# Attention with routing to experts: the written order inside a pair of heads, who empties PSUM, and the remainder keys' product with v as two tiles of 64 columns

## The chip, the cores and the metric

The kernel runs on one core of a Trainium2 chip. The core has TensorE (PE, with its weight loads listed apart as PEld), VectorE (DVE), ScalarE (ACT), GpSimd (POOL) and SyncE (SP), which issues most transfers. The metric is device microseconds of one launch, smaller is better.

## What is computed

Attention over 8 batches, 8 heads, 576 positions and head size 64 with a bias that a small network makes of positions; then each of the 4608 tokens goes to the one of 8 experts that a gate picks. Cut to what matters:

```python
scores = scale * q @ k.T + bias            # (8, 8, 576, 576)
attn = exp(scores - max); attn /= attn.sum(-1)
x = (attn @ v), heads side by side          # (4608, 512)
logits = x @ w_gate + modality_bias[modality_id]
e = argmax(logits); gate = softmax(logits)[e]
out = gate * (relu(x @ w1[e]) @ w2[e])
```

## The kernel before

**Stages.** A bias table is built first (to about 76 us of the span), then `attention()` works through 32 pairs of heads (4 pairs a batch) to about 643 us, then the experts' tiles follow. Beside the pairs runs the routing of the batch that is just done.

**A pair.** The 576 positions of a pair are 512 in four blocks of 128 rows for each of its two heads (units u = 0 to 3) and a remainder of 64 rows for each head, both heads together (u = 4). For each unit `scores` (L435) multiplies q with k in three terms of a split into a high and a low part. For u < 4 it works in tiles of 64 rows, one head in each, twelve products of 288 columns; for u = 4 in full rows, six. DVE adds the bias table and takes the row minimum (L449, the scores are negated), ACT takes the exponential in place (`exps`, L464), both from `Eb`, a ring of four tiles. `etrans` (L479, L485, L490) transposes the exponentials on PE into the PSUM banks `eps`, part 0 and part 1, and `take` copies them to `eT`. The columns 512 to 576 of a unit (the remainder keys) are copied together by POOL (`compact`, L469) and transposed by `rtrans` (L507) into `rT`. `prep` transposes q and k of a later pair (L403, and L408 with L409 for the remainders), and `take` writes them in a high (`ph0`, `ph1`, `ph2`) and a low part.

**The products with v.** `av(n, half, part)` makes one output of 128 rows (64 of each head) and 288 positions in two parts. The products with the 512 main keys (L527) are column tiles: 128 rows by 64 columns, one head in each, so two stand side by side. The remainder keys of both heads are the 128 rows of one product (L521), with `vrem`, a 128 by 128 matrix that has each head's v in its own corner and zeros elsewhere. It comes first in half 0 and last in half 1. In the trace each of these float32 products has two records, each transpose has one.

**What sets the order.** `ORDER` is written out by hand, one string for each unit. PE, ACT, DVE and POOL each take their instructions in that order. The letters: `S` scores; `e`, `f` the exponentials of the first and second head; `t`, `T` the two parts of `etrans` of the unit two before; `R` is `rtrans`; `a`, `A`, `b`, `c` the four parts of `av` for the pair before; `0`, `1`, `2` are `prep` of the next pair; `C` is `compact`; `X` and `B` are one step of routing with PE work and one without; `q`, `k` turn q and k of the pair after the next on POOL; `V`, `L` start loads on SP. A number behind a letter puts off its copies out of PSUM by so many letters (they also run when their bank is wanted again). `ON_ACT` names the copies that ACT makes; DVE makes the others.

Of the kernel before, what the change touches and what calls it, by code (L numbers as in the profile page):

```python
# [22 lines left out]
S = 576  # L23
# [87 lines left out]
class Attn:  # L111
# [205 lines left out]
        self.flush(lambda x: x[1] == ("x", self.n_x % 2))  # L317
        return self.xps[self.n_x % 2]

    ON_ACT = ("av0", "av1", "e01", "e20", "e21", "e30", "e31", "e40", "e41", "lt0", "lt1", "rT", "xr")  # L320

    def take(self, what, out, ps, scale=1.0):

# [6 lines left out]
    def take_now(self, what, out, ps, scale):  # L330

        if what[:2] == "pl":
            ps, hi = ps
            self.nc.vector.scalar_tensor_tensor(out, ps, scale, hi.bitcast(F32), op0=ALU.mult, op1=ALU.subtract)
        elif what in self.ON_ACT:
            self.nc.scalar.activation(out, ps, AF.Copy, scale=scale)  # L336
# [173 lines left out]
    def av(self, n, half, part):  # L510

        nc = self.nc
        if half == 0 and part == 0:
            self.xT[n] = self.xTb[n // NP % 2][:, n % NP, :]
        if part == 0:
            self.avps = self.xbank()
        v = self.vmain[n]
        sl = slice(HS * half, HS * half + HS)
        ps = self.avps[:, 0:HS]

        rem = lambda **kw: nc.tensor.matmul(ps, self.vrem[n % 2], self.rT[:, sl], skip_group_check=True, **kw)  # L521
        if half == 0 and part == 0:
            rem(start=True, stop=False)
        for k in (0, 1) if part == 0 else (2, 3):
            for h in range(2):
                o = slice(64 * h, 64 * h + 64)
                nc.tensor.matmul(  # L527
                    ps[o, :],
                    v[:, h, k, :],
                    self.eT[:, h, k, sl],  # L530
                    start=half == 1 and k == 0,
                    stop=half == 0 and k == 3,
                    tile_position=(0, 64 * h),
                    skip_group_check=True,
                )
        if part == 1:
            if half == 1:
                rem(start=False, stop=True)
            self.take(f"av{half}", self.xT[n][:, sl], ps)
            self.avps = None  # L540
            if half == 1:
                del self.vmain[n]

    def first_steps(self, route):
# [34 lines left out]


    ORDER = (
# [5 lines left out]
    )  # L587

    def attention(self):
# [889 lines left out]
```

## Time and profile before

| | |
|---|---|
| median of 3 runs | 1091.09 us (1089.97 to 1091.13) |
| the profiled execution | 1091.33 us, its span 1089.4 us |
| PE busy | 1066.4 us, 98% of the span |
| DVE, ACT, POOL busy | 736.7, 678.8, 246.6 us |
| granted clock of TensorE | 0.999 |

The span runs from the first to the last instruction; 1.9 us of the launch lie around it. Matmuls overlap, so a busy PE is read best from the starts of its groups: what a group costs is the time from its start to the start of the next one.

### The profile page before, as it was taken

The numbers are of one execution on the slowest core, as the hardware profiler recorded it, in microseconds if no ns is written. First come the engines' busy times: TensorE is split into PE (matmuls) and PEld (weight loads), VectorE is DVE, ScalarE is ACT, GpSimd is POOL, SyncE is SP. The second block draws the span as 40 slices with busy tenths as digits, with TensorE's granted clock in tenths as the row PEclk, the third lists the DMA queues.
The fourth block names the chain that finished last, engine by engine and source line by source line (L and its number), as shares of the span: only waits on it lengthen the run. The fifth ranks groups of instructions, "written<-read, shape, count | busy, mean of one in ns | idle before, by whom it ended". The sixth has DMA issues, their size and how long they took to land.

```text
span 1089.4 us, 23080 instructions
## 1 busy us (share of the span) xinstructions
PE 1066.4 (98%) x8580; PEld 842.9 (77%) x8580; DVE 736.7 (68%) x1580; ACT 678.8 (62%) x1333; POOL 246.6 (23%) x521
## 2 busy tenths in 40 slices
PE   6989999999999999999999999999999999999997
PEld 3456777777777777777776779999999999898986
DVE  7987768677686776766868756587455665545544
ACT  6776766767667667676676765654455554444544
POOL 1012222414224224142242221331110001101110
PEclk9999999999999999999999999999999999999999
DMA  5983412212212122222221511112113621151500
GB/s 164 219 192 116 144 43 77 69 56 74 69 52 92 54 67 69 55 84 60 56 88 49 201 45 40 59 64 70 58 49 117 240 100 52 38 215 48 195 31 32
DMA packets 71960, 98.19 MB, mean 90 GB/s; under 512 B 23054, under 2 KB 47886, under 8 KB 71842
## 3 DMA queue, kind: packets, MB, share of 16 engines
q1 hardware_dynamic: 65826, 77.62, 24.0%
q0 software_dynamic: 5920, 19.03, 4.8%
q8 instruction: 69, 1.13, 0.4%
q14 instruction: 49, 0.40, 0.1%
q10 hardware_dynamic: 96, 0.00, 0.0%
HBM read 135.62 MB, written 23.90 MB: 146 GB/s over the span
## 4 chain that ended last, share of the span: by engine, by line
PE 90%; DVE 1%; issue 1%; ACT 1%; POOL 0%; POOLq 0%; DVEq 0%; ACTq 0%
PE p L1200 18%; PE p L1217 18%; PE sps L435 14%; PE xps L527 13%; PE eps L479 10%; PE xps L521 4%; PE xps L403 3%; PE xps L872 2%; PE xps L1180 2%; PE xps L507 1%; PE eps L485 1%; PE xps L779 1%; PE xps L409 1%; DVE Eb L449 1%; PE p L1399 1%
## 5 line engine op out<-in xcount | busy, mean ns | idle before, releaser
L464 ACT ACTIVATE Eb<-Eb,mn 128x576 f32<-128x576 f32 x288 | 221.1, 770 | 37.2 <-DVE mn L449 36.8
L449 DVE CUSTOM_DVE_ANT_0 Eb<-sps,NBm 128x576 f32<-128x576 f32 x256 | 183.7, 755 | 83.2 <-PE sps L435 70.3
L435 PE MATMUL sps<-QK 64*128 64x288 f32 (+1 forms) x1728 | 172.8, 311 | 3.1 <-DVE mn L449 2.0
L435 PEld LDWEIGHTS sps<-QK 64*128 64x128 f32 (+1 forms) x1728 | 133.4, 185 | 44.3 <-DVE QK L338 16.4
L1200 PE MATMUL p<-QK,w1hi 128*128 128x256 f32 x1136 | 160.9, 284 | 0.0
L1203 DVE SCALAR_TENSOR_TENSOR hl<-p,hh 128x512 fp32r<-128x512 f32 x72 | 49.7, 691 | 154.5 <-ACT hh L1202 154.5
L527 PE MATMUL xps<-eT,vraw 128*64 128x288 f32 x1024 | 151.8, 418 | 0.0
L1200 PEld LDWEIGHTS p<-QK,w1hi 128*128 128x128 f32 x1136 | 147.0, 192 | 2.9 <-issue 1.8
L479 PE MATMUL eps<-idf,Eb 128*128 128x128 f32 x1024 | 143.9, 276 | 0.0
L479 PEld LDWEIGHTS eps<-idf,Eb 128*128 128x128 f32 x1024 | 115.6, 141 | 12.7 <-issue 5.7
L336 ACT ACTIVATE eT<-eps 128x512 f32<-128x512 f32 x192 | 106.6, 590 | 28.8 <-PE eps L479 15.2
L1202 ACT ACTIVATE hh<-p 128x512 fp32r<-128x512 f32 x72 | 43.0, 598 | 116.6 <-PE p L1200 112.6
L1217 PE MATMUL p<-w2hi,hh 128*128 128x512 f32 x288 | 114.2, 396 | 0.0
L1217 PE MATMUL p<-w2hi,hl 128*128 128x512 f32 x288 | 112.5, 391 | 0.0
L1226 POOL DMA_INDIRECT out<-mo,idt x36 | 38.5, 1069 | 322.4 <-ACT QK L1183 222.2
L469 POOL COPY rem<-Eb 128x128 f32<-128x128 f32 x128 | 37.8, 296 | 301.8 <-ACT Eb L464 226.4
L527 PEld LDWEIGHTS xps<-eT,vraw 128*64 128x64 f32 x1024 | 62.2, 136 | 53.5 <-issue 25.4
L1163 DVE TENSOR_TENSOR w2lo<-NBm,w2hi 128x1024 fp32r<-128x1024 f32 x72 | 88.2, 1225 | 16.2 <-ACT w2hi L1162 16.1
L1200 PE MATMUL p<-QK,w1lo 128*128 128x256 f32 x568 | 91.3, 283 | 0.0
L1163 DVE TENSOR_TENSOR w1lo<-NBm,w1hi 128x1024 fp32r<-128x1024 f32 x72 | 84.2, 1231 | 0.2 <-ACT w1hi L1162 0.2
L1225 ACT ACTIVATE mo<-p,gates 128x512 f32<-128x512 f32 x36 | 24.8, 689 | 89.1 <-PE p L1217 74.4
L1200 PEld LDWEIGHTS p<-QK,w1lo 128*128 128x128 f32 x568 | 78.3, 192 | 0.0
(221 smaller groups left out, 1685.7 us busy)
## 6 DMA issues: line engine op xcount, KB each, us to landing
NBm<-moe_w SPq DMA_DIRECT2D x23, 2048.0 KB
NBm<-moe_w SPq DMA_DIRECT2D x44, 1024.0 KB
NBr<-xg SPq DMA_DIRECT2D x20, 516.0 KB
NBm<-xTb SPq DMA_DIRECT2D x32, 288.0 KB
qraw<-q SPq DMA_DIRECT2D x32, 256.0 KB
kraw<-k SPq DMA_DIRECT2D x32, 256.0 KB
vraw<-v SPq DMA_DIRECT2D x32, 256.0 KB
xg<-blank SPq DMA_DIRECT2D x9, 516.0 KB
```

Source lines behind the costliest of these rows:

```text
L336: self.nc.scalar.activation(out, ps, AF.Copy, scale=scale)
L435: nc.tensor.matmul(self.sps[h][:, half, 0:HS], QK[o, q, qs], QK[o, k, HS * half : HS * half + HS], start=i == 0, stop=i == 2, skip_group_c ...
L449: nc.vector.tensor_tensor_reduce(out=e.rearrange("p (t w) -> p t w", t=2), in0=self.sps[h][:, :, 0:HS], in1=nb.rearrange("p (t w) -> p t w ...
L464: self.nc.scalar.activation(e, e, AF.Exp, bias=mn, scale=-1.0, accum_out=sm)
L479: nc.tensor.transpose(ps[:, k, :], e[:, part, P * k : P * k + P], self.idf)
L521: rem = lambda **kw: nc.tensor.matmul(ps, self.vrem[n % 2], self.rT[:, sl], skip_group_check=True, **kw)
L527: nc.tensor.matmul(ps[o, :], v[:, h, k, :], self.eT[:, h, k, sl], start=half == 1 and k == 0, stop=half == 0 and k == 3, tile_position=(0, ...
L1163: self.nc.vector.tensor_tensor(l, w, h.bitcast(F32), op=ALU.subtract)
L1200: nc.tensor.matmul(ps[:, a, :], w[:, c, fs], x[:, c, :], start=i == 0, stop=i == len(ops) - 1)
L1202: nc.scalar.activation(hh[:, sl, :], ps, AF.Relu)
L1203: nc.vector.scalar_tensor_tensor(hl[:, sl, :], ps, 0.0, hh[:, sl, :].bitcast(F32), op0=ALU.max, op1=ALU.subtract)
L1217: nc.tensor.matmul(ps, h[:, f, sl], m[:, f, :], start=i == 0, stop=i == len(ops) - 1)
```

## The change

Three things change. The remainder product is written as two column tiles of 64, as the other products with v are. `ORDER` has the letters in other places: in u = 0 and 1 `1` (L403) stands between `S` and `a` and no longer between `T` and `A`; `t` of the last unit stands before `S`; the routing steps `X` stand in u = 2, 3 and 4, of which none is ahead of `t` in u = 0 any more; `B` comes four times instead of five; `k` and `L` are a unit earlier and later, `V` a unit later. `ON_ACT` gives `e00`, `e11`, `ph0`, `ph1`, `ph2` to ACT and `e01`, `e31`, `e40`, `e41`, `lt0`, `xr` to DVE.

```diff
-    ON_ACT = ("av0", "av1", "e01", "e20", "e21", "e30", "e31", "e40", "e41", "lt0", "lt1", "rT", "xr")
+    ON_ACT = ("av0", "av1", "e00", "e11", "e20", "e21", "e30", "lt1", "ph0", "ph1", "ph2", "rT")
...
-        rem = lambda **kw: nc.tensor.matmul(ps, self.vrem[n % 2], self.rT[:, sl], skip_group_check=True, **kw)
+        def rem(**kw):
+            for h in range(2):
+                o = slice(64 * h, 64 * h + 64)
+                nc.tensor.matmul(
+                    ps[o, :], self.vrem[n % 2][:, o], self.rT[:, sl], tile_position=(0, 64 * h), skip_group_check=True, **kw
+                )
...
     ORDER = (
-        "S X B t R1 T3 f e C L",
-        "01 t3 S a T 11 A f e C",
-        "S B t2 X e f k C q T2",
-        "b S e c B t1 T2 f V C",
-        "S B X 2 t T e B",
+        "S B t 01 R1 e f T2 C",
+        "t1 S 12 L a k T1 f B e C A2",
+        "q S t1 e T2 X B f C b",
+        "B S c1 e T X f t C",
+        "B S 2 t2 V T2 X e",
     )
```

On PE, in u = 1 of a pair in the middle, the first half of the products with v stood like this between two units' scores:

```order
L435 MATMUL sps_724<-QK_73 128x288
L521 MATMUL xps_78<-rT,vrem_110 128x288
L527 MATMUL xps_78<-eT,vraw_3687 64x288 x4
L490 MATMUL eps_726<-idf,Eb 64x64 x2
L403 MATMUL xps_77<-idf,qks_109 128x128 x4
L527 MATMUL xps_78<-eT,vraw_3687 64x288 x4
L435 MATMUL sps_723<-QK_73 128x288
```

Now it stands like this (the products' line is L533 now, the remainder's L524):

```order
L435 MATMUL sps_724<-QK_73 128x288
L403 MATMUL xps_78<-idf,qks_109 128x128 x4
L524 MATMUL xps_77<-rT,vrem_110 64x288 x2
L533 MATMUL xps_77<-eT,vraw_3732 64x288 x4
L490 MATMUL eps_726<-idf,Eb 64x64 x2
L533 MATMUL xps_77<-eT,vraw_3732 64x288 x4
L435 MATMUL sps_723<-QK_73 128x288
```

The transposes of k (L403) moved ahead of the products, which now run in column tiles from the remainder to the last one.

On PE, in u = 3, the end of the second half and what follows up to the remainder rows' scores (six products of L435 in a row) was this:

```order
L435 MATMUL sps_724<-QK_73 128x288
L527 MATMUL xps_77<-eT,vraw_3687 64x288 x4
L521 MATMUL xps_77<-rT,vrem_110 128x288
L479 MATMUL eps_725<-idf,Eb 128x128 x4
L479 MATMUL eps_726<-idf,Eb 128x128 x4
L435 MATMUL sps_723<-QK_73 128x288 x6
L872 MATMUL xps_78<-idf,xTb_94 128x128 x4
L408 MATMUL xps_77<-idf,krem_3771 128x64
```

and is this now (L878 was L872):

```order
L435 MATMUL sps_724<-QK_73 128x288
L533 MATMUL xps_77<-eT,vraw_3732 64x288 x4
L524 MATMUL xps_77<-rT,vrem_110 64x288 x2
L479 MATMUL eps_726<-idf,Eb 128x128 x4
L878 MATMUL xps_78<-idf,xTb_94 128x128 x4
L479 MATMUL eps_725<-idf,Eb 128x128 x4
L435 MATMUL sps_723<-QK_73 128x288 x6
L408 MATMUL xps_77<-idf,krem_3818 128x64
```

The routing's transposes (L872) moved from behind the scores to between the two parts of `etrans`, whose parts changed places.

On DVE, at the end of the first pair after a batch, the minimum of the last unit (`mn_4_0`), two routing steps (L803, L811, then L818 to L821) and the remainder's high and low parts (L338 and L334 on `QK_72`) stood like this ahead of the next pair's first minimum (`mn_0_0`):

```order
L449 ISA Eb,mn_4_0_3700<-sps_723,NBr 128x576
L449 ISA mn_4_0_3700 128x1
L803 TENSOR_TENSOR lw_3631<-xps_77,rec 128x64
L811 TENSOR_REDUCE lgs_3704<-lw_3631 128x40
L338 CAST QK_72<-xps_78 128x192
L334 SCALAR_TENSOR_TENSOR QK_72<-xps_78,QK_72 128x192
L818 TENSOR_TENSOR lgs_3704<-lgs_3704,mbias 128x40
L820 TENSOR_REDUCE mx_3722<-lgs_3704 128x5
L821 TENSOR_TENSOR lgs_3704<-lgs_3704,mx_3722 128x40
L449 ISA Eb,mn_0_0_3738<-sps_723,NBm 128x576
```

and now (L809 was L803, L817 was L811):

```order
L449 ISA Eb,mn_4_0_3722<-sps_723,NBr 128x576
L449 ISA mn_4_0_3722 128x1
L334 SCALAR_TENSOR_TENSOR QK_72<-xps_77,QK_72 128x192
L809 TENSOR_TENSOR lw_3702<-xps_78,rec 128x64
L817 TENSOR_REDUCE lgs_3743<-lw_3702 128x40
L449 ISA Eb,mn_0_0_3760<-sps_723,NBm 128x576
```

The remainder's low part moved ahead of the routing, its high part left DVE, and L818 to L821 went behind the next unit's minima.

## Rows read from the trace of the kernel before

**Rows 1.** Busy time by engine from 300 to 400 us, PE clock, DMA share, GB/s.

```profile
core 0: us, PE busy (x) PEld busy (x) DVE busy (x) ACT busy (x) POOL busy (x), PEclk, DMA share, GB/s
300.00:400.00 100.00, 99.82 (x857) 73.33 (x856) 74.59 (x203) 69.75 (x167) 29.72 (x64) 1.00 0.22 64
```

**Rows 2.** Waits of PE from 100 to 690 us: total, times, longest.

```profile
PE xps L507 <- DVE QK L1184: 1.6, 1, 1.6
PE sps L435 <- DVE QK L338: 0.5, 1, 0.5
```

**Rows 3.** Timeline of PE, one pair: start us, length, line, operation, tiles, rows*columns.

```profile
402.61 1.06 PE L435 MATMUL sps<-QK 64*128 64x288 f32 x12
403.59 0.75 PE L521 MATMUL xps<-rT,vrem 128*128 128x288 f32 x2
404.27 1.19 PE L527 MATMUL xps<-eT,vraw 128*64 128x288 f32 x8
405.30 0.28 PE L490 MATMUL eps<-idf,Eb 128*64 128x64 f32 x4
405.51 0.66 PE L403 MATMUL xps<-idf,qks 128*128 128x128 f32 x4
406.10 1.19 PE L527 MATMUL xps<-eT,vraw 128*64 128x288 f32 x8
407.22 1.06 PE L435 MATMUL sps<-QK 64*128 64x288 f32 x12
408.21 0.66 PE L479 MATMUL eps<-idf,Eb 128*128 128x128 f32 x4
408.70 0.60 PE L872 MATMUL xps<-idf,xTb 128*128 128x128 f32 x4
409.14 0.60 PE L479 MATMUL eps<-idf,Eb 128*128 128x128 f32 x4
409.67 1.19 PE L527 MATMUL xps<-eT,vraw 128*64 128x288 f32 x8
410.79 1.07 PE L435 MATMUL sps<-QK 64*128 64x288 f32 x12
411.78 1.19 PE L527 MATMUL xps<-eT,vraw 128*64 128x288 f32 x8
412.90 0.75 PE L521 MATMUL xps<-rT,vrem 128*128 128x288 f32 x2
413.49 1.04 PE L479 MATMUL eps<-idf,Eb 128*128 128x128 f32 x8
414.29 1.03 PE L435 MATMUL sps<-QK 128*128 128x288 f32 x6
```

**Rows 4.** Timeline of PE in the last pair but one, without L403 between the products.

```profile
621.54 0.28 PE L490 MATMUL eps<-idf,Eb 128*64 128x64 f32 x4
621.66 1.14 PE L527 MATMUL xps<-eT,vraw 128*64 128x288 f32 x8
622.73 1.06 PE L435 MATMUL sps<-QK 64*128 64x288 f32 x12
```

**Rows 5.** The page's group of weight loads of the products with v: busy, mean ns.

```profile
L527 PEld LDWEIGHTS xps<-eT,vraw 128*64 128x64 f32 x1024 | 62.2, 136 | 53.5 <-issue 25.4
```

**Rows 6.** Timeline of PE, then of DVE, at the first pair after a batch.

```profile
164.90 1.55 PE L435 MATMUL sps<-QK 64*128 64x288 f32 x12
...
164.60 0.74 DVE L811 TENSOR_REDUCE lgs<-lw 128x40 f32<-128x320 f32 x1
165.64 0.36 DVE L334 SCALAR_TENSOR_TENSOR QK<-xps,QK 128x192 fp32r<-128x192 f32 x1
```

**Rows 7.** DVE's minima and a copy out of PSUM; ACT's copy by the page.

```profile
408.45 0.76 DVE L449 CUSTOM_DVE_ANT_0 Eb<-sps,NBm 128x576 f32<-128x576 f32 x1 [0.83 <-PE sps L435]
409.81 0.69 DVE L338 COPY eT<-eps 128x512 f32<-128x512 f32 x1
...
L336 ACT ACTIVATE eT<-eps 128x512 f32<-128x512 f32 x192 | 106.6, 590 | 28.8 <-PE eps L479 15.2
```

## The prediction

> **What bounds the kernel now.** I read the busy shares by stage first, then what PE waits for, then PE's groups in order of time. In a stretch of the pairs' stage PE is busy 99.8 of 100 us, DVE 74.6, ACT 69.8 and POOL 29.7 [rows 1]. Busy PE proves little, since ends of matmuls overlap, but from 100 to 690 us PE waits 2.1 us in all [rows 2]. So until about 643 us the time is the sum of the steps from one PE group's start to the next, and a cut there comes back in full as long as DVE and ACT empty the banks in time. The experts' stage that follows is not touched; it starts that much earlier.
>
> In the timeline of a pair [rows 3] the reader should see that a group's step depends on its neighbours. Four transposes in full rows take 0.44 us between other transposes (408.70 to 409.14), 0.49 when they come after the 64-row scores (408.21 to 408.70), 0.53 when column tiles come after them (409.14 to 409.67). So to enter another kind of tile costs 0.05, to leave it 0.09. The eight records of a part of the products with v show the same: 1.12 with a change on both sides (409.67 to 410.79), 1.03 with one at the entry alone (404.27 to 405.30; the L490 behind them is a column tile too), 1.07 with one at the exit alone [rows 4]. Without a change they take 0.97, which is 0.49 for two neighbouring tiles of 288 columns (four records).
>
> **The remainder and the order, first half.** Before, from the remainder's start to the next scores: 0.68 (remainder) + 1.03 + 0.21 (L490) + 0.59 (L403) + 1.12 = 3.63 us, from 403.59 to 407.22 [rows 3]. Of five changes of tile kind in it, three stay: scores to L403, L403 to the products, products to scores. Now: L403 between two changes 0.59 (its own row, 405.51 to 406.10); remainder as two tiles 0.49, and the first part 0.97, entered with one change 0.05; L490 between column tiles 0.12; the second part with its exit 1.07 [rows 4]. Sum 3.29; saved 0.34.
>
> **Second half.** Before: 1.12 + 0.59 = 1.71 us, 411.78 to 413.49 [rows 3]. Now the part and the remainder share one entry and one exit, 1.12 + 0.49 = 1.61, and the transposes behind them enter from another kind, 0.05 more: 1.66. Saved 0.05. The price of the two remainder tiles is the one thing here that no row shows, since no row has two tiles that stream the same rows. From below it is bounded by the 0.49 of two tiles of this shape, from above by two products one after the other, each at the old price: 0.59 less one entry is 0.54, so 1.08. I take 0.49: same rows, columns, type and tile places as the products beside it.
>
> A rule speaks against it. The eight records of one part need eight weight loads of 136 ns, 1.09 us together [rows 5], and the whole part takes 0.97, so loads run beside column tiles' products. The Trainium skill, in "TensorE: Matmul & The Clock Gate", part 3 (packing small matmuls), says that weight loads overlap with matmuls in flight only where the row group differs, and column tiles of 128 rows share theirs. By that the part could not be shorter than its loads and products together, so the trace disagrees; were the rule to hold for the added loads alone, the time would be that of the fourth rival.
>
> **Sum of the tiles.** 0.39 us in each round that has L403 and the products, thirty of them: 11.7. The last two rounds have no L403; there the first half was 0.68 + 1.03 + 0.12 + 1.07 = 2.90 and becomes 0.05 + 0.49 + 0.97 + 0.12 + 1.07 = 2.70, and with the second half that is 0.25 twice, 0.5. Together 12.2 us.
>
> **What else moves on PE costs nothing.** The routing's transposes (L872) and the first part of the last unit's `etrans` stay inside runs of full-row work, so no change of kind comes or goes; L408 now follows the remainder rows' scores directly and the X behind it stands among transposes, 0.44 for 0.44.
>
> **The wait after a batch.** In the first pair after a batch the first scores take 1.55 instead of 1.06, 0.49 more [rows 6]. It comes seven times, six in that form and once as the recorded wait of 0.5 [rows 2], 3.4 us together. Its second half of columns needs the remainder keys' low part; that stood on DVE behind a routing reduction of 0.74 and ended only at 166.0 [rows 6]. Now it stands ahead of that reduction, its high part is on ACT, and PE has one more routing group in front of those scores, so this wait goes. Next to be late are the routing's nine small operations for the one-hot rows: they now stand ahead of the third unit's minima, and the rank products behind them on PE need them. That can give back between nothing and the same 0.49. Between these ends I take half: 1.7 us gained, 3.4 and 0 for the range.
>
> **Copies that change engine.** ACT hands over three copies of 512 columns, the small one of 64 and, in some pairs, routing rows; it takes over four of 512 and the remainder's high part. At 590 ns by the group's mean [rows 7] that is a trade of about 2.7 us against 2.7 in a pair of 18; DVE, at 0.69 a copy [rows 7], does the reverse. Both have a quarter of the time free [rows 1], so load costs nothing; what could cost is the place. The tightest that I find is the end of u = 3: DVE makes two minima, a routing copy (`xr`, new there) and the copy of bank 0, and PE wants that bank again for the first transposes after L409. Laid out from the rows, with the scores' start as zero: minima from 1.23 to 2.6 (408.45 stands 1.23 after 407.22); the routing's transposes end near 3.7 (0.99 + 1.61 + 0.49 + 0.60), its copy near 4.4, bank 0's copy near 5.1. PE wants the bank at 0.99 + 1.61 + 0.49 + 0.44 + 0.36 + 0.96 + 0.37 = 5.2 (0.36 is half of 413.49 to 414.29 less the shorter step into the scores; 0.96 and 0.37 are the remainder scores and L408 with L409). About 0.1 in hand in pairs with such a copy, 0.3 or more in the others. I price it at nothing.
>
> **SP and POOL.** The loads keep their order on SP, all sent about a pair ahead of use. `k` now asks for its rows a unit sooner; if POOL waits there, `compact` for the next unit stands behind it, which PE wants only in the next pair. At POOL's 30% [rows 1] I price it at nothing. In the table stage the first pair's three high parts go from DVE to ACT, at most 3 x 0.59 either way; taken as nothing, with 1.7 us in the range.
>
> **How the numbers follow.** The sum is made against the profiled execution, 1091.33 us: less 12.2 and 1.7 is 1077.4. The median lies 0.24 below that execution, so the forecast is **1077.2 us**.
>
> First, the forecast: PE stays the bound and the steps add up. Its own range is 1074 (all of the 3.4 us) to 1081 (none of it and some lateness). Chance 0.72.
>
> Second, the copies' places. If PE waits 0.2 us for bank 0 in every pair, 6.4 us go back: 1083.6, with 1081 to 1087 for a little less or more. For: the 0.1 us that I count in hand. Against: it holds only for pairs with a routing copy there. Chance 0.14.
>
> Third, the price of a change of kind is not a price of the change, but of which group stands next, and L403's move gives nothing. Then only the remainder's 0.54 to 0.49 is left, 64 times, 3.2 us, with 1.7 for the batches: 1086.2. Against: the same 0.05 and 0.09 come out of transposes and products alike. Chance 0.05.
>
> Fourth, on the other side: the two remainder tiles don't stand side by side, because both stream the same rows of `rT`. At 1.08 a pair for 0.49 this costs 0.59 x 64 = 38 us: 1115. It makes the kernel slower as soon as two tiles cost over 0.74, since (1093.3 - 1077.2) / 64 is 0.25. For: no row shows shared rows. Against: the products beside them differ in nothing else. Chance 0.04. With exposed weight loads, 4 x 0.136 x 64 = 35 us, it would be 1112; the 0.97 of a part speaks against that. Chance 0.02. The Trainium skill's sentence on row groups, named above, is this last case.
>
> The rest, 0.03, is a wait that I don't see and that eats the gain. That the change isn't made as told is out: the listing of PE shows two products of 64 rows out where there was one of 128.
>
> About 0.2% is what a measurement of this kernel can tell from no change, 1088.9 to 1093.3. Faster 0.90, the same 0.04, slower 0.06. Range: 1074 to 1086; it leaves out the third rival's upper edge, the fourth and the rest.
>
> **What would show it.** After: a pair's first half takes 3.29 from L403's start to the next scores, with L490 at 0.12; the two remainder tiles take 0.49 more than the part beside them; first scores after a batch take 1.06; PE still waits only a few us; the experts' stage lasts as long as before. The forecast is wrong if transposes after L409 start late, or if the remainder's step is over 0.7.

## The result and the profile after

| | before | after |
|---|---|---|
| median | 1091.11 us (1089.97 to 1091.89) | 1077.20 us (1076.62 to 1077.33) |
| profiled execution, its span | 1091.33 us, 1089.4 us | 1076.62 us, 1074.8 us |
| PE busy | 1066.4 us | 1054.4 us |
| DVE, ACT, POOL busy | 736.7, 678.8, 246.6 us | 737.3, 675.7, 250.3 us |

After takes 0.9869 of the time of before, 95% interval 0.9857 to 0.9882: 13.9 us less. The forecast was 1077.2.

PE is still what the time goes by. First the same two views as in [rows 1, 2], of after: the busy times from 300 to 400 us (length, then PE, PEld, DVE, ACT and POOL, then granted clock, DMA share and GB/s), and what PE waited for from 100 to 690 us (total, times, longest).

```profile
300.00:400.00 100.00, 99.97 (x906) 75.32 (x906) 76.51 (x208) 72.15 (x172) 32.15 (x67) 1.00 0.25 72
```

```profile
PE xps L857 <- DVE ohb L843: 0.4, 1, 0.4
PE xps L1186 <- DVE QK L1190: 0.2, 1, 0.2
PE eps L479 <- DVE eT L338: 0.2, 1, 0.2
```

PE stays busy all the time and waits 0.8 us where it waited 2.1, while every other engine has a little more to do in 100 us, because the same work goes through in less time. Next, PE's groups in order of time in one pair after, to be laid beside [rows 3] (start, us, engine, line, operation, out and in, rows by columns of the tile, records):

```profile
389.80 0.27 PE L408 MATMUL xps<-idf,krem 64*128 64x64 f32 x1
...
395.88 0.66 PE L403 MATMUL xps<-idf,qks 128*128 128x128 f32 x4
396.46 0.71 PE L524 MATMUL xps<-rT,vrem 128*64 128x288 f32 x4
397.00 1.14 PE L533 MATMUL xps<-eT,vraw 128*64 128x288 f32 x8
397.97 0.28 PE L490 MATMUL eps<-idf,Eb 128*64 128x64 f32 x4
398.08 1.14 PE L533 MATMUL xps<-eT,vraw 128*64 128x288 f32 x8
399.16 1.05 PE L435 MATMUL sps<-QK 64*128 64x288 f32 x12
...
403.71 1.19 PE L533 MATMUL xps<-eT,vraw 128*64 128x288 f32 x8
404.73 0.66 PE L524 MATMUL xps<-rT,vrem 128*64 128x288 f32 x4
405.32 0.66 PE L479 MATMUL eps<-idf,Eb 128*128 128x128 f32 x4
405.81 0.60 PE L878 MATMUL xps<-idf,xTb 128*128 128x128 f32 x4
...
407.57 0.27 PE L408 MATMUL xps<-idf,krem 64*128 64x64 f32 x1
```

By starts, the first half takes 0.58 (L403) + 0.54 (remainder) + 0.97 (part) + 0.11 (L490) + 1.08 (part with its exit) = 3.28 us, from 395.88 to 399.16; before it was 3.63. The second half takes 1.02 + 0.59 = 1.61, and the transposes behind it take 0.49 (405.32 to 405.81) instead of 0.44: 1.66 for 1.71. So a pair is 0.35 + 0.05 = 0.40 shorter.

**A batch.** The starts of L408 mark the pairs. Four of them in a row lay 17.89, 18.18, 18.27 and 17.68 apart before, 72.02 together; after it is 17.41, 17.77 (the two L408 rows above), 16.89 and 18.16, 70.23 together. Single pairs shift because the routing steps stand elsewhere. A batch is 1.79 shorter, of which 4 x 0.40 = 1.60 are the tiles; the other 0.19 are about what is left of the wait after a batch. That wait went from the place where it was, and a smaller lateness came further on. First PE at the first scores after a batch, then PE at the place of the new wait in that batch and in a later one:

```profile
162.79 1.07 PE L435 MATMUL sps<-QK 64*128 64x288 f32 x12
163.79 0.66 PE L479 MATMUL eps<-idf,Eb 128*128 128x128 f32 x4
...
172.86 0.18 PE L857 MATMUL xps<-ohb,ones 128*128 128x48 bf16 x1 [0.36 <-DVE ohb L843]
...
383.36 0.19 PE L856 MATMUL xps<-ohb,tri 128*128 128x48 bf16 x1
383.56 0.18 PE L857 MATMUL xps<-ohb,ones 128*128 128x48 bf16 x1
...
384.79 1.23 PE L435 MATMUL sps<-QK 64*128 64x288 f32 x12
385.94 1.19 PE L533 MATMUL xps<-eT,vraw 128*64 128x288 f32 x8
```

And DVE in the first of these batches:

```profile
171.29 1.52 DVE L843 TENSOR_TENSOR ohb<-ohb,oh 128x8 bf16<-128x8 bf16 x5
172.76 0.76 DVE L449 CUSTOM_DVE_ANT_0 Eb<-sps,NBm 128x576 f32<-128x576 f32 x1
```

The first scores after the batch last 1.07 now where they lasted 1.55 [rows 6]; by starts that is 1.00 (162.79 to 163.79) for 1.48, in the middle of the run 0.99 for 1.49: 0.50 gained. The rank products L856 and L857 wait for the one-hot rows of L843: from the transposes ahead of them to the products behind them it is 1.24 (382.43 to 383.67) where it was 1.11 before. And the minimum stands on DVE behind those rows, so the scores after it take 1.15 (384.79 to 385.94) instead of 0.98. That gives back 0.13 + 0.17, and 0.20 of the 0.50 are left.

**Where the rest is.** The second L408 starts at 77.3 instead of 76.3 (the table stage with the first pair is 1.0 longer), from there to the last L408 it is 523.0 instead of 537.8 (14.8 shorter), and from there to the end 474.5 instead of 475.3 (0.8 shorter). Together 14.6, which is the spans' difference. Of the 14.8, 12.0 are the tiles (30 x 0.40), 1.1 come from the first pair after the table stage, in which the scores had waited 0.85 us for a minimum (L449) on DVE and no longer do, and the 1.7 left fall to the pairs with routing: 0.2 in a batch in the middle, more in the last one.

### The profile page after: what moved, and what is told of

It is laid out like the page before. It is cut to its first block, busy times and chain, and to the rows that moved or that the text cites. A ratio compares the mean times of both kernels' runs of the same rounds, so it can differ in the third digit from the quotient of the medians.

```text
span 1074.8 us, 23294 instructions
## 1 busy us (share of the span) xinstructions
PE 1054.4 (98%) x8708; PEld 838.5 (78%) x8708; DVE 737.3 (69%) x1596; ACT 675.7 (63%) x1317; POOL 250.3 (23%) x521
## 3 DMA queue, kind: packets, MB, share of 16 engines
q8 instruction: 70, 1.15, 0.4%
## 4 chain that ended last, share of the span: by engine, by line
PE 90%; DVE 1%; ACT 1%; issue 0%; POOL 0%; POOLq 0%; ACTq 0%; DVEq 0%
PE p L1206 19%; PE p L1223 18%; PE sps L435 14%; PE xps L533 12%; PE eps L479 11%; PE xps L524 3%; PE xps L403 3%; PE xps L878 2%; PE xps L1186 2%; PE eps L485 1%; PE xps L507 1%; PE xps L785 1%; PE xps L409 1%; PE xps L408 1%; PE p L1405 1%; PE p L1383 1%
## 5 line engine op out<-in xcount | busy, mean ns | idle before, releaser
L449 DVE CUSTOM_DVE_ANT_0 Eb<-sps,NBm 128x576 f32<-128x576 f32 x256 | 183.7, 755 | 85.8 <-PE sps L435 45.0
L435 PE MATMUL sps<-QK 64*128 64x288 f32 (+1 forms) x1728 | 170.5, 309 | 0.7 <-DVE mn L449 0.6
L435 PEld LDWEIGHTS sps<-QK 64*128 64x128 f32 (+1 forms) x1728 | 133.3, 185 | 44.4 <-issue 10.2
L533 PE MATMUL xps<-eT,vraw 128*64 128x288 f32 x1024 | 147.1, 412 | 0.0
L479 PE MATMUL eps<-idf,Eb 128*128 128x128 f32 x1024 | 146.7, 278 | 0.2 <-DVE eT L338 0.2
L479 PEld LDWEIGHTS eps<-idf,Eb 128*128 128x128 f32 x1024 | 112.7, 141 | 24.6 <-issue 18.8
L336 ACT ACTIVATE eT<-eps 128x512 f32<-128x512 f32 x160 | 94.4, 590 | 24.7 <-PE eps L479 17.8
L533 PEld LDWEIGHTS xps<-eT,vraw 128*64 128x64 f32 x1024 | 65.3, 137 | 42.3 <-issue 9.5
L338 DVE COPY eT<-eps 128x512 f32<-128x512 f32 x128 | 87.5, 684 | 11.5 <-PE eps L479 11.5
```

The lines of the kernel that those rows point to most:

```text
L338: self.nc.vector.tensor_copy(out, ps)
L435: nc.tensor.matmul(self.sps[h][:, half, 0:HS], QK[o, q, qs], QK[o, k, HS * half : HS * half + HS], start=i == 0, stop=i == 2, skip_group_c ...
L449: nc.vector.tensor_tensor_reduce(out=e.rearrange("p (t w) -> p t w", t=2), in0=self.sps[h][:, :, 0:HS], in1=nb.rearrange("p (t w) -> p t w ...
L479: nc.tensor.transpose(ps[:, k, :], e[:, part, P * k : P * k + P], self.idf)
L533: nc.tensor.matmul(ps[o, :], v[:, h, k, :], self.eT[:, h, k, sl], start=half == 1 and k == 0, stop=half == 0 and k == 3, tile_position=(0, ...
```

## The experiments

Each edit is made to the kernel named. The medians of before in the same sessions were 1090.91 to 1091.46.

**The parts apart.** First before with the remainder as two tiles and its old order (rem_only):

```diff
-        rem = lambda **kw: nc.tensor.matmul(ps, self.vrem[n % 2], self.rT[:, sl], skip_group_check=True, **kw)
+        def rem(**kw):
+            for h in range(2):
+                o = slice(64 * h, 64 * h + 64)
+                nc.tensor.matmul(
+                    ps[o, :], self.vrem[n % 2][:, o], self.rT[:, sl], tile_position=(0, 64 * h), skip_group_check=True, **kw
+                )
```

> The kernel before with only the remainder product as two column tiles; order and copies as before. If a change of tile kind costs 0.14 us (0.05 in, 0.09 out): first half 0.05 + 0.49 + 0.97 + 0.21 + 0.59 + 1.12 = 3.43 instead of 3.63, second half 1.66 instead of 1.71, 0.25 in each of 32 rounds, 8.0 us: 1083.1. If the price belongs to the neighbours and not to the change: 0.05 for each of 64 products, 3.2 us: 1087.9. If two tiles that stream the same rows cost more than 0.49, it shows here as over 1083.

Measured 1083.10 us, ratio 0.9929 (0.9915 to 0.9942): 7.8 us gained. PE's first half in a pair runs from the remainder to the next scores:

```profile
399.24 0.71 PE L524 MATMUL xps<-rT,vrem 128*64 128x288 f32 x4
...
402.67 1.06 PE L435 MATMUL sps<-QK 64*128 64x288 f32 x12
```

3.43 for 3.63. With the 0.05 of the second half this is 0.25 in each of 32 rounds, 8.0. The third rival, in which the tiles alone would bring 3.2, is out.

Then after with the remainder as one product again (order_only):

```diff
-        def rem(**kw):
-            for h in range(2):
...
+        rem = lambda **kw: nc.tensor.matmul(ps, self.vrem[n % 2], self.rT[:, sl], skip_group_check=True, **kw)
```

> The changed kernel with the remainder as one product of 128 columns again; new order and new copies stay. By the price of a change of kind: the remainder now follows L403, both in full rows, so 0.49 + 0.63 + 1.02 + 0.12 + 1.07 = 3.33 instead of 3.63, 0.30 in 30 rounds, 9.0 us, and 1.7 for the waits after a batch: 1080.4. So the two parts would give 8.0 and 10.7 alone and 13.9 together, because both take away the same change of kind. If the parts were independent, it would be 13.9 - 8.0 = 5.9: 1085.2. If the price belongs to the neighbours: 1089.4.

Measured 1078.53 us, ratio 0.9888 (0.9873 to 0.9903). PE in a pair (the products' lines are L521 and L527 again):

```profile
396.28 0.66 PE L403 MATMUL xps<-idf,qks 128*128 128x128 f32 x4
396.78 0.65 PE L521 MATMUL xps<-rT,vrem 128*128 128x288 f32 x2
397.36 1.19 PE L527 MATMUL xps<-eT,vraw 128*64 128x288 f32 x8
...
399.57 1.05 PE L435 MATMUL sps<-QK 64*128 64x288 f32 x12
...
405.23 0.75 PE L521 MATMUL xps<-rT,vrem 128*128 128x288 f32 x2
405.82 0.60 PE L479 MATMUL eps<-idf,Eb 128*128 128x128 f32 x4
```

The first half is 3.29, the same as in after; the second is 1.71 for 1.66. So in the new order the two tiles are worth 0.05 a round, 1.6 us, and 1.3 were measured; I had expected 3.2. The rows say why: behind L403, another group in full rows, the one product takes 0.58, which is 0.49 and an exit of 0.09. Its own price is 0.49 and not 0.54. What makes it dear in before is its entry from 64-row scores or from column tiles, which costs 0.10 (0.68 = 0.10 + 0.49 + 0.09, and 405.23 to 405.82 = 0.59 = 0.10 + 0.49). In the second half there is one change of kind either way, and the 0.05 is that entering the transposes costs 0.05 where entering the product costs 0.10. The parts alone gain 7.8 and 12.4, together 13.9: each takes away some of the same changes of kind.

Then after with the old list of ACT's copies (copies_as_before):

```diff
-    ON_ACT = ("av0", "av1", "e00", "e11", "e20", "e21", "e30", "lt1", "ph0", "ph1", "ph2", "rT")
+    ON_ACT = ("av0", "av1", "e01", "e20", "e21", "e30", "e31", "e40", "e41", "lt0", "lt1", "rT", "xr")
```

> The changed kernel with the list of ACT's copies as before (e00, e11, ph0 to ph2 on DVE; e01, e31, e40, e41, lt0, xr on ACT). If the trade of copies is worth nothing by itself, 1077.2 within 1 us. If the new order needs it (PE waits for a bank or for the high parts), later: the wait after a batch comes back, up to 3.4 us, or 0.2 in each pair, 6.4 us: 1080.6 to 1083.6. If ACT's high parts are what the table stage lost (the first L408 starts 0.8 us later than before): about 0.8 earlier, 1076.4.

Measured 1078.08 us, ratio 0.9883 (0.9868 to 0.9898). Four pairs take 70.24, as in after, so the trade between the engines is worth nothing in the steady stretch. The median is 0.9 more than after's; between the profiled runs it is 1.5, of which 0.7 lie in the last two pairs, 18.48 and 17.52 for 18.28 and 17.06, and 0.7 behind the last L408. The first L408 comes at 35.6, 1.2 earlier than in after, but by the third L408 (93.8 in both) that is gone. The ratios' intervals overlap.

**L403's place.** To put L403 back between the parts of the products, I first moved its letter behind `k` (k_back, from after):

```diff
-        "t1 S 12 L a k T1 f B e C A2",
+        "t1 S L a k T1 12 f B e C A2",
```

> The changed kernel with the transposes of k (L403) back between L490 and the second part of the products. By the price of a change of kind: 0.05 + 0.49 + 0.97 + 0.21 + 0.59 + 1.12 = 3.43 instead of 3.29, 0.14 in 30 rounds, 4.3 us: 1081.5. If the price belongs to the neighbours, or if only the waits count: 1077.2.

Measured 1100.36 us, ratio 1.0081 (1.0068 to 1.0095). Behind `k`, L403 transposes the rows that POOL has just turned for a later pair, so its scores are not those of the pair. PE waits for POOL there (L403 for L391, 17.7 us over the span, eleven times), so the run doesn't price L403's place. With L403 ahead of `k` it does (k_back_first, from after):

```diff
-        "t1 S 12 L a k T1 f B e C A2",
+        "t1 S L a T1 12 k f B e C A2",
```

> The changed kernel with L403 back between L490 and the second part of the products, ahead of the turn of the next k on POOL (the run k_back had it behind, so L403 read the rows of a later pair and waited for POOL). By the price of a change of kind: first half 3.43 instead of 3.28, 0.15 in 30 rounds, 4.4 us: 1081.6. If the price belongs to the neighbours: 1077.2.

Measured 1087.70 us, ratio 0.9963 (0.9950 to 0.9977): 10.5 more than after, where one change of kind more was to cost 4.4. PE's first half, then the first row of its waits, then DVE ahead of that wait:

```profile
404.64 0.71 PE L524 MATMUL xps<-rT,vrem 128*64 128x288 f32 x4
...
408.07 1.06 PE L435 MATMUL sps<-QK 64*128 64x288 f32 x12
```

```profile
PE xps L857 <- DVE ohb L843: 4.9, 7, 1.1
```

```profile
389.20 0.69 DVE L334 SCALAR_TENSOR_TENSOR QK<-xps,QK 128x512 fp32r<-128x512 f32 x1 [0.75 <-ACT QK L336]
...
390.73 1.52 DVE L843 TENSOR_TENSOR ohb<-ohb,oh 128x8 bf16<-128x8 bf16 x5
```

The half is 3.43, just as priced (0.15 in thirty rounds, 4.5 us). The rest is not TensorE's doing: k's low part on DVE waits 0.75 for its high part on ACT, the one-hot operations stand behind it, and the rank products wait for these once a batch, 4.9 us in all where it was 0.4; another 2.9 are lost in the first pair (43.33 between its L408 and the next, for 40.46). With the 4.5 of the tiles that makes 11.9 of the 12.7 between the two profiled runs. So L403's new place gains by the changes of kind and also by having k's parts ready early.

**The wait after a batch, alone** (before_rem_first, from before): the remainder's transposes ahead of the routing step in the last unit.

```diff
-        "S B X 2 t T e B",
+        "S B 2 X t T e B",
```

> The kernel before, with one pair of letters exchanged in u = 4: the preparation of the remainders (2) ahead of the routing step X. If the wait in the first scores after a batch is for the remainder keys' low part behind the routing's reduction on DVE, it goes, seven times 0.49, 3.4 us: 1087.6, and PE's first scores after a batch take 1.06. If that wait has another cause (the bank of the scores, the routing itself): 1091.0 and 1.55 still.

Measured 1090.29 us, ratio 0.9992 (0.9983 to 1.0001): no change. PE at the first scores after a batch, and in another pair of the batch:

```profile
166.80 1.07 PE L435 MATMUL sps<-QK 64*128 64x288 f32 x12
167.80 0.66 PE L479 MATMUL eps<-idf,Eb 128*128 128x128 f32 x4
...
218.70 0.33 PE L409 MATMUL xps<-idf,qrem 128*128 128x128 f32 x1
218.96 1.06 PE L779 MATMUL xps<-xTb,wgb 128*32 128x512 f32 x8
219.95 1.09 PE L479 MATMUL eps<-idf,Eb 128*128 128x128 f32 x8
```

The wait goes (the scores last 1.07 for 1.55), which shows its cause: the low part's place on DVE behind the routing. But the gate's products (L779, tiles of 32 columns) now stand between two groups in full rows, with an entry and an exit of their own, and the pair that holds them takes 18.70 where the one that held them took 18.28; in the pair behind it k's transposes come 0.38 or more after L490 instead of 0.21 (one of these is listed as a wait of 0.2 for DVE). Four pairs take 71.82 for 72.02, so 0.20 a batch are left, and the first pair takes 2.0 longer.

**Further along the same line.** If changes of kind are what counts, one more pair of them can go: L408 is itself a 64-row tile, and would be cheaper behind 64-row scores than behind the remainder rows' full-row scores. Four kernels move `2` there. r64_beside_scores, from after:

```diff
-        "q S t1 e T2 X B f C b",
+        "q S 2 t1 e T2 X B f C b",
...
-        "B S 2 t2 V T2 X e",
+        "B S T2 V t2 X e",
```

> The changed kernel with the preparation of the remainders moved from u = 4 to u = 2 right behind the scores, and T ahead of t in u = 4. L408 works in tiles of 64 rows as the scores do, so two changes of kind go (13 to 11 in a pair), 0.28 in 31 pairs, 8.7 us: 1068.5. If the price belongs to the neighbours, or if waits for a bank take the place: 1077 or more.

Measured 1090.03 us, ratio 0.9991 (0.9982 to 1.0000). The first row of PE's waits, and the place in a pair:

```profile
PE xps L533 <- DVE QK L334: 14.9, 20, 1.5
```

```profile
388.26 1.07 PE L435 MATMUL sps<-QK 64*128 64x288 f32 x12
389.16 0.21 PE L408 MATMUL xps<-idf,krem 64*128 64x64 f32 x1
389.31 0.33 PE L409 MATMUL xps<-idf,qrem 128*128 128x128 f32 x1
...
392.05 1.19 PE L533 MATMUL xps<-eT,vraw 128*64 128x288 f32 x8 [1.48 <-DVE QK L334]
```

The scores' step falls from 0.98 to 0.90 and L408's from 0.20 to 0.15 as hoped, but the products get the bank that L408 and L409 filled, because the routing step behind them has the other one, and PE stands until DVE has copied it. Another 4.1 us go to eleven waits of the transposes (L479) for ACT's copies of `eT`. This is the second rival's mechanism, a bank wanted before its copy, at another place and a larger size.

r64_and_k does the same and also puts `12` ahead of `S` in u = 1:

```diff
-        "t1 S 12 L a k T1 f B e C A2",
-        "q S t1 e T2 X B f C b",
+        "t1 12 S L a k T1 f B e C A2",
+        "q S 2 t1 e T2 X B f C b",
...
-        "B S 2 t2 V T2 X e",
+        "B S T2 V t2 X e",
```

> The same with the transposes of k (L403) moved ahead of the second unit's scores, into the run of full-row transposes in u = 0 and 1. One more change of kind goes, 0.14 in 30 pairs, 4.2 us: 1064.3, less what PE waits for the bank that L403 then takes over from the other preparation 1.3 us before it (high part 0.6 and low part 0.7 have to be out: 0 to 0.3 in a pair, up to 9 us, which would make it slower than the run before).

Measured 1096.38 us, ratio 1.0047 (1.0033 to 1.0061). The wait of L533 for DVE's low part stays (13.7 us, 20 times), and L403 now waits 29 times for the same kind of copy, 4.5 us together.

r64_x_apart takes the routing step out of u = 2, so that the banks don't meet:

```diff
-        "q S t1 e T2 X B f C b",
+        "q S 2 t1 e T2 B f C b",
...
-        "B S 2 t2 V T2 X e",
+        "B S X t2 V T2 X e",
```

> As r64_beside_scores, but the routing step X of u = 2 stands in u = 4 ahead of the transposes, and these keep their order (t, T). In r64_beside_scores the first products of the second half waited 14.9 us for the low part on DVE, since X had taken the other bank; here these products take the other bank themselves. If the price of a change of kind holds and that bank was the loss, up to 8.7 us below the changed kernel: 1068.5, with 2 or 3 us back where no X stands between the scores and t in u = 4: 1071. If moving the remainders' preparation loses for another reason: 1077 or more.

Measured 1087.23 us, ratio 0.9963 (0.9949 to 0.9978). Three of the four pairs of a batch take 17.55, 16.88 and 17.36 us, but the fourth 19.2 to 21.2, where after's longest is 18.28. PE's routing transposes of the remainder (L507) wait for DVE seven times, 13.7 us in all. PE at the first of these, then DVE ahead of it:

```profile
203.33 1.08 PE L507 MATMUL xps<-idf,rem 128*128 128x128 f32 x4 [1.91 <-DVE xrb L338]
204.21 1.06 PE L479 MATMUL eps<-idf,Eb 128*128 128x128 f32 x4
205.06 1.06 PE L485 MATMUL eps<-idf,Eb 128*128 128x128 f32 x4
206.05 1.40 PE L435 MATMUL sps<-QK 64*128 64x288 f32 x12
```

```profile
202.59 0.68 DVE L338 COPY xrb<-xps 64x512 f32<-64x512 f32 x1 [3.43 <-DMA xg<-xrb,pos]
```

With two of the three routing steps in one unit (u = 4), they follow each other so closely that the ring of two buffers for the routed rows (`xrb`) is still being sent when DVE needs the next; DVE waits, and PE behind it. That is about 2 us once a batch, and behind the first of the seven waits the clock takes nearly as much again (last section).

r64_x_early is made from setup_dve below and spreads the routing steps over u = 1 and u = 4:

```diff
-        "t1 S 12 L a k T1 f B e C A2",
-        "q S t1 e T2 X B f C b",
+        "t1 X S 12 L a k T1 f B e C A2",
+        "q S 2 t1 e T2 B f C b",
...
-        "B S 2 t2 V T2 X e",
+        "B S X t2 V T2 e",
```

> setup_dve with the remainders' preparation behind the scores of u = 2, as in r64_x_apart, but the three routing steps spread over u = 1 (ahead of the scores), 3 and 4 (ahead of t). In r64_x_apart two steps in one unit wanted a routing row's buffer (two in a ring) before its transfer had left, PE waited for it once in four pairs, and lost some 2 to 4 us each time; three of four pairs took 0.5 us less than in the changed kernel. If spreading the steps ends that wait, two changes of kind less in 31 pairs, 8.7 us: 1066.9. If the routing step ahead of the scores makes the transposes of k or the products wait for a bank (0.15 to 0.3 in most pairs): 1070 to 1075. Over 1075.6 would mean that the place in u = 4 can't be given up, whatever the routing does.

Measured 1075.20 us (1074.74 to 1075.91), ratio 0.9851 (0.9835 to 0.9868), which is not told apart from setup_dve. The large waits are gone, but PE in a pair shows where the gain went:

```profile
391.27 0.60 PE L485 MATMUL eps<-idf,Eb 128*128 128x128 f32 x4
392.02 0.66 PE L878 MATMUL xps<-idf,xTb 128*128 128x128 f32 x4 [0.16 <-DVE QK L334]
```

L485's step is 0.75 instead of 0.44, because the routing's transposes want the bank that `0` filled (it stands in u = 0 since the change, in u = 1 before) and DVE has its low part still to copy. The 0.28 won on tiles are given back as 0.31 in such pairs; four pairs take 70.0 for 70.23.

**The first pair's high parts** (setup_dve, from after): they are made by DVE in the first pair, as in before, and by ACT in all later ones.

```diff
-            self.take(f"ph{part}", hi, o, sc)
+            self.take(f"ph{part}" if n else f"hp{part}", hi, o, sc)
```

> The changed kernel with the first pair's three high parts, which are made in the table stage, on DVE again. If they are what made the first two L408 start 0.8 and 1.0 us later than before, 1 us: 1076.2. If the table stage only shifts work that the first pairs then wait for: 1077.2.

Measured 1075.60 us (1075.25 to 1076.01), ratio 0.9852 (0.9837 to 0.9866), 1.6 less than after; the ratios' intervals overlap a little. The first L408 comes at 35.9 instead of 36.8. That much holds in every profiled execution: the seven kernels that make these copies on ACT have it at 36.6 to 37.3, the six that make them on DVE at 35.6 to 36.4. But at the second L408 only 0.44 of the 0.9 is left (76.84 for 77.28), and that is within what kernels with the same table stage differ by: order_only, which has after's, comes at 76.88, and rem_only, which has before's, at 76.82 where before has 76.32. The next 0.35 come in the first batch, where after's wait of 0.36 for the one-hot rows is missing here; the last L408 is at 599.5 instead of 600.3, and the profiled runs differ by 0.8 us. So the three copies on ACT make the first L408 later, and whether the table stage as a whole loses by them is not shown. Which wait they lengthen is open: PE's longest for ACT there (L198, for the copy at L187) is 5.6 us in after and 5.5 here. The edit's size is near what runs can tell, but both kernels that have it are the fastest of the study, and both lie below after's lowest run.

## Why the prediction was right, point by point

- **PE is the bound and a cut on it comes back in full.** Right. PE waits 0.8 us in the stage, and 0.40 a pair in the timeline (0.39 forecast) is 0.40 a pair in the starts of L408 (16.88 before and 16.48 after in the pairs without routing).
- **First half 3.63 to 3.29.** Right: 3.28 in after. The price of a change of kind is a price of the change and not of the neighbour: k_back_first moved L403 alone and got the 0.15 back to the hundredth, rem_only took 0.20 without moving it. The third rival (1086.2) is refuted. The Trainium skill, "TensorEngine Tiling (Array Packing)", section "Key Properties", says that a change of tiling mode makes TensorE drain, without a figure. The traces agree in that each change costs time, 0.05 to 0.10 us on either side of it and 0.15 to 0.19 in all, but they don't show a drain as such.
- **Second half 1.71 to 1.66, the two remainder tiles at 0.49.** Right: 0.54 with an entry of 0.05, 0.59 with an exit of 0.10 (404.73 to 405.32). Two tiles that stream the same rows stand side by side, and four weight loads don't show in the time. The fourth rival is out in both its forms (1115, 1112). The Trainium skill, "TensorE: Matmul & The Clock Gate", part 3, has weight loads overlap with matmuls in flight only where the row group differs. For these tiles the trace disagrees: the two take 0.49 besides their entry while their four loads of 0.137 us come to 0.55.
- **The one product's own price.** This step was wrong, and it cost nothing only because the total was read from whole halves. I split its 0.59 in the second half into an entry of 0.05 and 0.54 of work; order_only shows 0.10 and 0.49. So the two tiles are no cheaper than the one product: all that they save is a change of kind in the old order's first half, and a cheaper one in the second half. By my split the order alone would have left 3.2 us to the tiles, and the run left 1.3.
- **The wait after a batch: between 0 and 3.4, taken as 1.7.** Right in size (0.2 in a batch in the middle, 1.7 over all pairs with routing) and in mechanism: the first wait went, as 1.07 for 1.55 shows, and the rank products behind the one-hot operations became late, as written.
- **Copies between ACT and DVE: nothing.** Right for the steady stretch, where the run with the old list has the same four pairs to 0.01. The tight place at the end of u = 3 held: PE waited for such a bank once, 0.2 us, so the second rival (1083.6) did not come about. How near it was is told by r64_beside_scores and r64_x_early, where a bank that is not yet copied decides.
- **SP and POOL: nothing.** Nothing was seen of them in after. r64_x_apart shows that the sending of routed rows, which POOL starts, is the next to be late when routing steps move closer.
- **The table stage: up to 1.7 either way, taken as nothing.** Within its bounds: after's second L408 is 1.0 later than before's, but kernels with the same table stage differ there by 0.4 to 0.5 between runs, so that how much of the 1.0 is the change's is open. The first pair behind it gained 1.1 that the sum didn't have (the scores' wait of 0.85 for L449). These two nearly cancel. That the total came out to the tenth is luck: the sum was made for the profiled execution and gave 1077.4 where 1076.62 was measured, and after's median happens to lie 0.6 above its profiled execution where before's lay 0.2 below. The sum was good to about 1 us, not better.

## What to carry to other kernels

Where TensorE never waits, the price of its work hangs on which kind of tile stands next to which: read each group's step with and without a change of kind, and order the work so that groups of one kind stand together, before looking for cheaper products. Count the changes that an edit takes away only once: two edits that remove the same change do not add up. And once such an order is tight, the next cut is decided by who empties the banks and how close together routing steps come, not by TensorE: of four attempts to go on, three lost more to waits for a copy or a buffer than the tiles could save, and one broke even.

## What the runs showed of the hardware

Two things I had not expected. The price of a change depends on what is entered and on what is left. By the steps above, to enter costs 0.05 us into transposes and into column tiles, and 0.10 into the one remainder product of 128 columns; to leave costs 0.09 to 0.10 out of each of the three. Between the transposes and that product, both in full rows, nothing was paid (0.58 = 0.49 and the exit).

And a wait of TensorE can cost twice, but mostly did not. In r64_x_apart, the stretches around the first wait, of 1.91 us, and around the last, of 2.82 (columns as in [rows 1]):

```profile
201.00:203.30 2.30, 0.42 (x4) 0.18 (x2) 0.71 (x2) 1.08 (x2) 0.33 (x3) 1.00 0.28 100
203.30:206.00 2.70, 2.67 (x12) 2.39 (x12) 2.62 (x6) 1.96 (x5) 2.17 (x3) 0.52 0.26 98
...
629.23:631.73 2.50, 0.00 (x1) 0.01 (x1) 0.74 (x2) 0.78 (x2) 0.71 (x3) 1.00 0.16 63
631.73:634.43 2.70, 2.70 (x24) 2.23 (x26) 1.05 (x2) 1.18 (x2) 2.12 (x3) 1.00 0.26 98
```

At the first, TensorE was busy for 0.42 of 2.30 us, and in the 2.7 us after it the granted clock is 0.52, about the lower of its two levels, 1.2 of 2.4 GHz. The groups there take 0.88, 0.85, 0.99 and 1.33 us by their starts (L507 to the step of L435, the last from the next group at 207.38), where in after they take 0.44, 0.44, 0.53 and 0.99: 1.65 us lost on top of the 1.91 waited. At the last, TensorE did next to nothing for 2.5 us, and the clock after it is 1.00. So it is behind the five waits between them, of 1.51 to 2.20 us. The length of the wait alone doesn't tell which one is followed by the lower clock; what does stays open.
